# Fifteen small loads on ScalarE's DMA queue in a one-core decode layer

## The chip, the core and the metric

The kernel runs on one core of a Trainium2 chip. The metric is the device time of one execution in microseconds, as the median of the runs shown. A profiled execution has a time of its own, and a span (first to last instruction of the core) that is a little shorter.

## The reference, cut to what matters

One decode step of a transformer layer with adaptive layer norm, batch 2, width 640: attention with 32 heads of 192 over the last 1024 of 4096 cached positions, then a gated feed-forward of width 1536. Everything is bfloat16 in memory.

```python
mod = (silu(c) @ w_mod).reshape(2, 6, 1, 640)
sa, ca, ga, sb, cb, gb = (mod[:, i] for i in range(6))
h = layernorm(x) * (1 + ca) + sa
q = (h @ wq)                      # 32 heads x 192
p = softmax(q . k[-1024:] * 192 ** -0.5)
x = x + ga * ((p . v[-1024:]) @ wo)
h = layernorm(x) * (1 + cb) + sb
x = x + gb * ((gelu(h @ w_gate) * (h @ w_up)) @ w_down)
```

The cached keys and values that it reads are 50 MB, the weights some 27 MB; each byte is used once.

## The kernel before, in words

The program builds one list of operations for each engine (`_Sched`) and works out the waits from what each operation reads and writes. Within an engine the order is the order in which operations are added to its list. Line 257 (`k_dma`) is the one helper that issues every DMA, so all issues carry L257.

SyncE's list holds all large loads: w_mod, wq in two pieces, then the keys and values, then wo in four, w_gate, w_up in two, w_down in three pieces, and last the store of the output. Keys and values go through `ring`, five slots of 128 partitions x 24,576 bytes (64 of the 256 positions that a partition holds; a head occupies four partitions). The order of the 16 ring loads is the list `items`: four of k for batch 0, then v of batch 0 and k of batch 1 in turn, then v of batch 1. `declare_ring` puts a slot's next load into SyncE's list once the operation that empties the slot is in its own.

ScalarE's list begins with the two small loads of c into `cc` and x into `xc` (8 rows of 320 bytes each, L268 and L269), then silu of `cc` (L347), the evacuation of the modulation and of q. Line 434 is the last step of q: the copy of the selected q from PSUM into `qbc`, which the helper `move` records at L419. ScalarE's next operation after it is the exponential of the first softmax (L487), with the load of its function table before it.

After `qbc`, DVE multiplies each half slot of keys by q in place (L448), TensorE sums over parts of the head's width with an identity matrix (L459), DVE finishes the row sums (L468). `softmax` (L472 to L492) is a short chain over all engines. `d_mask` (L496) spreads the probabilities, `p_pv` (L508) multiplies them by the values. wo (L601), the second layer norm, w_gate and w_up (L617) and w_down (L638) follow, then two DVE operations (L644, L646) and the store. `filler` (L441) runs matmuls whose result nobody reads.

`sp_tail` at the end of SyncE's list waits for the store of the output.

Of the kernel before, what the change touches and what calls it, by code (L numbers as in the profile page):

```python
# [6 lines left out]
ACTF = mybir.ActivationFunctionType  # L7
# [96 lines left out]
def bass_adaLN_cond__sliding_block_cached__geglu_ffn__decode_kernel(  # L104
# [63 lines left out]
    with es:  # L168
        S = _Sched(nc, es)
# [35 lines left out]
        cc = sb("cc", [P, DN], BF16)  # L205
        sc = sb("sc", [P, DN], BF16)
# [21 lines left out]
        esum = sb("esum", [P, 2], F32)  # L228
        rden = sb("rden", [P, 2], F32)
        On = sb("On", [P, 2, Dh], BF16)  # L230
        ps = es.enter_context(nc.psum_tensor("ps", [P, 8, 512], F32))

        BK_T = 2
# [8 lines left out]
        def bank(k):  # L242
            return ("bank", k)
# [8 lines left out]
        sem_wd = [S.sem("d_wd%d" % i) for i in range(len(WD_SPLIT))]  # L252
        sem_ring = [S.sem("d_ring%d" % i) for i in range(NS)]
        sem_out = S.sem("d_out")

        def k_dma(dst, src):
            return lambda e: e.dma_start(dst, src)  # L257
# [5 lines left out]
        def dram_rows(v):  # L263
# [11 lines left out]
             reads=[("S", 0, 0), ("S", 0, 1), ("S", 1, 0), ("S", 1, 1)], writes=["ident_f"], name="ident_f")  # L275
        S.op("pool", lambda e: e.tensor_copy(out=ident_b[:, :], in_=ident_f[:, :]),
             reads=["ident_f"], writes=["ident_b"], name="ident_b")
# [3 lines left out]
             reads=["ident_f"], writes=["G32"], name="G32")  # L281
        S.op("dve", lambda e: e.tensor_reduce(out=M32[:, :], in_=ident_f[:, :].rearrange("p (h t) -> p h t", t=QP), axis=AX.X, op=ALU.add),
             reads=["ident_f"], writes=["M32"], name="M32")
        S.op("dve", lambda e: e.tensor_copy(out=M32b[:, :], in_=M32[:, :]), reads=["M32"], writes=["M32b"], name="M32b")
        S.op("dve", lambda e: e.tensor_copy(out=Bsel[:, :].rearrange("p (a m) -> p a m", m=SQ),
                                            in_=G32[:, :].unsqueeze(1).broadcast_to([P, NJ, SQ])),
             reads=["G32"], writes=["Bsel"], name="Bsel")

        S.op("dve", lambda e: e.tensor_copy(out=DS[:, :].rearrange("p (a m) -> p a m", m=SQ),
                                            in_=M32[:, :].unsqueeze(1).broadcast_to([P, NJ, SQ])),  # L290
             reads=["M32"], writes=["DS"], name="DS")


        for b in range(2):
            S.op("dve", (lambda b: lambda e: e.tensor_copy(
                out=SEL[:, b, :, BS * b:P:SQ], in_=G32[:, :].rearrange("p (j m) -> p m j", m=HM)))(b),
                reads=["G32"], writes=["SEL"], name="SEL%d" % b)
        for b in range(2):
            for m in range(HM):
                S.op("dve", (lambda b, m: lambda e: e.tensor_copy(  # L300
                    out=Qsel[:, b, m, :].rearrange("p (a m t) -> p a m t", a=NJ, m=HM)[:, :, m, :],
                    in_=ident_f[:, BS * b:P:SQ].unsqueeze(2).broadcast_to([P, NJ, QP])))(b, m),
                    reads=["ident_f"], writes=[("ring", 4, 0)], name="Qsel%d%d" % (b, m))
# [4 lines left out]
        def ring_keys(slot):  # L308
            return [half_key(slot, 0), half_key(slot, 1)]

        keep = {}
# [17 lines left out]
        def declare_ring(*consumed, upto=len(items)):  # L329
            ring_state["done"].update(place[it] for it in consumed)  # L330
            while ring_state["next"] < upto and (ring_state["next"] < NS or (ring_state["next"] - NS) in ring_state["done"]):
                n = ring_state["next"]
                kind, b, t = items[n]
                slot = n % NS
                cache = A_v_cache if kind == "v" else A_k_cache
                S.dma("sp", k_dma(ring[:, slot, :, :].rearrange("p j d -> p (j d)"),
                                  cache[b, :, K0:Sk, :].rearrange("h (q r) d -> h q r d", q=QP)[:, :, J * t:J * (t + 1), :].rearrange("h q r d -> h q (r d)")),
                      sem_ring[slot], writes=ring_keys(slot), name="ld_%s%d_%d" % (kind, b, t))
                ring_state["next"] += 1
# [4 lines left out]
        def to_contraction(dst, src, n, reads, writes, name):  # L344
            S.op("dve", lambda e: e.transpose(dst, src.rearrange("p (q k) -> p k q", k=n)), reads=reads, writes=writes, name=name)  # L345

        S.op("act", lambda e: e.activation(out=sc[:, :], in_=cc[:, :], func=ACTF.Silu), reads=["cc"], writes=["sc"], name="silu")  # L347
        to_contraction(scT[:, :, :], sc[:, :], KT, ["sc"], ["scT"], "scT")
        S.op("dve", lambda e: e.tensor_copy(out=X2[:, 0, :], in_=xc[:, :]), reads=["xc"], writes=[("X2", 0)], name="x_f32")  # L349

# [66 lines left out]
        def move(eng, dst, src, reads, writes, name):  # L417
            if eng == "act":
                S.op("act", lambda e: e.activation(out=dst, in_=src, func=ACTF.Copy), reads=reads, writes=writes, name=name)  # L419
            else:  # L420
                S.op("dve", lambda e: e.tensor_copy(out=dst, in_=src), reads=reads, writes=writes, name=name)  # L421
# [11 lines left out]
        S.op("pe", f, reads=[("qC", c) for c in range(NQC)] + ring_keys(4), writes=[bank(BK_O)], name="qsel")  # L433
        move("act", qbc[:, :, :].rearrange("p b d -> p (b d)"), ps[:, BK_O, 0:2 * Dh], [bank(BK_O)], ["qbc"], "qbc")
        declare_ring()

        def filler(n=1):
            def f(e):
                last = None
                for _ in range(n * ND):  # L440
                    last = e.matmul(ps[:, BK_W, 0:2 * Dh], lhsT=ident_b[:, :], rhs=qbc[:, :, :].rearrange("p b d -> p (b d)"),  # L441
                                    start=True, stop=True)
                return last
            S.op("pe", f, reads=["ident_b", "qbc"], writes=[bank(BK_W)], name="warm")
# [94 lines left out]
        steps = [(b, t, hf) for b in range(2) for t in range(NTL) for hf in range(2)]  # L539
# [29 lines left out]
        for i, nt in enumerate(OT_SPLIT):  # L569
            S.op("dve", (lambda t0, nt: lambda e: e.transpose(oT[:, t0:t0 + nt, :], oc.rearrange("p (q k) -> p k q", k=NT)[:, t0:t0 + nt, :]))(t0, nt),  # L570
                 reads=[("oc", c) for c in range(NQC)], writes=[("oT", t) for t in range(t0, t0 + nt)], name="oT%d" % i)
# [4 lines left out]
        for i, (ta, tb) in enumerate(wo_of):  # L576
# [5 lines left out]
              writes=["wg"], deps=r3_dead, name="ld_wg")  # L582
# [13 lines left out]
        for i, (ta, tb) in enumerate(wo_of):  # L596
            def f(e, ta=ta, tb=tb):
# [9 lines left out]
             reads=[bank(BK_M), ("modC", 0)], writes=[("lnt", 0)], name="ga_attn")  # L607
        S.op("dve", lambda e: e.tensor_tensor(out=X2[:, 0, :], in0=lnt[:, 0, :], in1=X2[:, 0, :], op=ALU.add),
             reads=[("lnt", 0)], writes=[("X2", 0)], name="x1")
        layer_norm("ln2", 1, 3)  # L610

        def ffn_gu(bk, wv, key, name, ka, kb):
            def f(e):
# [10 lines left out]
             reads=[bank(BK_G[0])], writes=["gl"], name="gelu")  # L624
        k0 = 0
        for ci, nk in enumerate(WU_SPLIT):
# [3 lines left out]
             reads=[bank(BK_G[1]), "gl"], writes=["aC"], name="geglu")  # L630
        to_contraction(aT[:, :, :], aC[:, :], FT, ["aC"], ["aT"], "aT")
        f0 = 0
        for ci, nf in enumerate(WD_SPLIT):
            def f(e, f0=f0, nf=nf):
# [10 lines left out]
             reads=[bank(BK_C), ("modC", 1)], writes=[("lnt", 1)], name="gb_y")  # L645
        S.op("dve", lambda e: e.tensor_tensor(out=sc[:, :], in0=lnt[:, 1, :], in1=X2[:, 0, :], op=ALU.add),  # L646
             reads=[("lnt", 1), ("X2", 0)], writes=["sc"], name="outC")
        S.dma("sp", k_dma(dram_rows(out[:, 0, :]), rows_of(sc)), sem_out, reads=["sc"], name="st_out")

        with nc.Block() as block:  # L650
            def sp_tail(e):
                e.wait_ge(sem_out, 16)

            @block.sync
            def _(e):
                S.emit("sp", e, tail=sp_tail)

            @block.gpsimd
            def _(e):
                S.emit("pool", e)  # L660

            @block.scalar
            def _(e):
                S.emit("act", e)

            @block.vector
            def _(e):
                S.emit("dve", e)

            @block.tensor  # L670
            def _(e):
                S.emit("pe", e)
# [28 lines left out]
```

## Time and profile before

| what | us |
|---|---|
| median of 3 runs | 189.07 (188.91 to 189.26) |
| the profiled execution | 188.59 |
| its span | 186.9 |
| DVE busy | 107.2 |
| PE busy | 121.0 |
| ScalarE busy | 13.9 |
| median from issue to landing, a ring load of keys | 29.6 |
| the same, a ring load of values | 25.3 |

The span moved 77.01 MB at a mean of 412 GB/s. Busy shares are means over stages with different limits; the DMA row of the slices, 40 slices of 4.67 us, tells for each stage whether loads were under way on all engines. Records of single DMA packets give a start, a duration, a size and a queue, but not which of the 16 DMA engines carried them; where one engine's packets are told apart below, it is because each starts where the one before it ended.

### The profile page before, as it was taken

To read this page: it belongs to the slowest core of one execution; us is meant where nothing else is said; L and a number is where in the kernel's file an instruction comes from. 1 tells how busy PE (TensorE), PEld (TensorE's weight loads), DVE (VectorE), ACT (ScalarE), POOL (GpSimd) and SP (SyncE) were. 2 spreads that over 40 slices of the span, in tenths; PEclk is the share of its full clock that TensorE was granted. 3 is DMA by queue.
4 is the path that set the end of the run, shared out by engine and by line. 5 is a ranking of instruction groups with operands and counts; after the bars stand their busy time and mean duration, and the time that the engine had idled before them with its cause. 6 is when DMAs were issued, how large, how long until landed. Compare 5 with 4: busy or idle time off the path is not lost.

```text
span 186.9 us, 2216 instructions
## 1 busy us (share of the span) xinstructions
PE 121.0 (65%) x982; PEld 60.5 (32%) x982; DVE 107.2 (57%) x114; ACT 13.9 (7%) x24; POOL 4.9 (3%) x12
## 2 busy tenths in 40 slices
PE   0004543565999889449999939929529997255442
PEld 0001221251343334125454513504225664244111
DVE  6802500029599998389599298288475612903331
ACT  2003200031000000000000000000010002400400
POOL 8100000000000000000000000000000000000000
PEclk9999999555699999966999997987957999955555
DMA  7999999999999999999999999999999999999980
GB/s 263 395 474 426 402 434 424 421 437 447 437 426 428 421 419 426 437 437 442 437 424 416 421 431 431 431 435 442 426 426 421 425 423 434 420 415 427 412 367 24
DMA packets 4220, 77.01 MB, mean 412 GB/s; under 512 B 500, under 2 KB 500, under 8 KB 1140
## 3 DMA queue, kind: packets, MB, share of 16 engines
q1 hardware_dynamic: 4188, 76.88, 96.6%
q8 instruction: 7, 0.11, 0.2%
q10 hardware_dynamic: 24, 0.01, 0.0%
q14 instruction: 1, 0.01, 0.0%
HBM read 76.88 MB, written 0.00 MB: 411 GB/s over the span
## 4 chain that ended last, share of the span: by engine, by line
DMA 48%; PE 27%; DVE 21%; SPq 2%; issue 1%; ACT 1%; DVEq 0%
DMA ring<-in_A_k_cache_dram 34%; DVE ring L448 14%; DMA ring<-in_B_w_down_dram 13%; PE ps L508 11%; PE ps L459 11%; PE ps L441 3%; DVE Sg L468 3%; DVE Em L496 2%; SPq L257 2%; ACT E_sb L487 1%; PE ps L638 1%; PE ps L489 1%; DVE M L474 0%; PE ps L483 0%; DVE gm L478 0%
## 5 line engine op out<-in xcount | busy, mean ns | idle before, releaser
L448 DVE TENSOR_TENSOR ring<-ring,qbc 128x6144 bf16<-128x6144 bf16 x16 | 53.5, 3351 | 10.8 <-DMA ring<-in_A_k_cache_dram 10.8
L459 PE MATMUL ps<-ring,ident_b 128*128 128x512 bf16 x192 | 49.8, 415 | 11.2 <-DVE ring L448 11.2
L459 PEld LDWEIGHTS ps<-ring,ident_b 128*128 128x128 bf16 x192 | 19.3, 105 | 38.9 <-DVE ring L448 15.4
L508 PE MATMUL ps<-ring,Em 128*64 128x384 bf16 x256 | 26.1, 365 | 4.9 <-DVE Em L496 4.9
L496 DVE TENSOR_TENSOR Em<-E_sb,M32b 128x2048 bf16<-128x2048 bf16 x8 | 18.2, 2282 | 4.0 <-PE ps L508 4.0
L508 PEld LDWEIGHTS ps<-ring,Em 128*64 128x64 bf16 x256 | 15.4, 122 | 14.9 <-DVE Em L496 6.4
L441 PE MATMUL ps<-qbc,ident_b 128*128 128x384 bf16 x88 | 18.1, 335 | 0.7 <-ACT qbc L419 0.7
L468 DVE TENSOR_REDUCE Sg<-ps 128x32 f32<-128x512 f32 x16 | 11.0, 687 | 8.8 <-PE ps L459 8.8
L388 PE MATMUL ps<-ring,scT 128*32 128x480 bf16 x40 | 4.4, 601 | 15.0 <-DMA ring<-in_w_mod_dram 15.0
L411 PE MATMUL ps<-r,hT 128*32 128x384 bf16 x80 | 6.7, 518 | 8.7 <-DMA r<-in_A_wq_dram 8.7
L441 PEld LDWEIGHTS ps<-qbc,ident_b 128*128 128x128 bf16 x88 | 8.1, 100 | 9.8 <-issue 4.5
L421 DVE CAST ring<-ps 128x384 bf16<-128x384 f32 x4 | 2.0, 553 | 15.4 <-PE ps L411 14.5
L601 PE MATMUL ps<-r,ring 128*32 128x160 bf16 x192 | 5.9, 304 | 5.8 <-DMA r<-in_A_wo_dram 3.0
L601 PEld LDWEIGHTS ps<-r,ring 128*32 128x32 bf16 x192 | 5.1, 128 | 6.6 <-DMA r<-in_A_wo_dram 3.6
L411 PEld LDWEIGHTS ps<-r,hT 128*32 128x32 bf16 x80 | 3.0, 140 | 12.4 <-issue 6.1
L522 ACT ACTIVATE On<-ps,rden 32x192 bf16<-32x192 f32 x4 | 1.6, 412 | 71.0 <-PE ps L508 61.4
L388 PEld LDWEIGHTS ps<-ring,scT 128*32 128x32 bf16 x40 | 1.3, 132 | 16.3 <-DVE X L349 14.9
L526 DVE TENSOR_SCALAR On<-ps,rden 32x192 bf16<-32x192 f32 x4 | 1.7, 418 | 7.4 <-ACT On L522 7.4
L617 PE MATMUL ps<-ring,hT 128*32 128x384 bf16 x40 | 3.7, 519 | 3.3 <-DVE hT L345 2.6
L570 DVE STREAM_TRANSPOSE ring<-ring 128x512 bf16<-128x512 bf16 x3 | 4.1, 1430 | 0.1
L606 DVE TENSOR_TENSOR lnt<-ps,modC 128x160 f32<-128x160 f32 x1 | 0.3, 325 | 6.5 <-PE ps L601 6.5
L487 ACT ACTIVATE E_sb<-Sg,nb 128x256 bf16<-128x256 f32 x2 | 1.0, 508 | 40.7 <-DVE nb L486 40.7
(68 smaller groups left out, 57.2 us busy)
## 6 DMA issues: line engine op xcount, KB each, us to landing
ring<-in_A_k_cache_dram SPq DMA_DIRECT2D x8, 3072.0 KB, 29.6
ring<-in_A_v_cache_dram SPq DMA_DIRECT2D x8, 3072.0 KB, 25.3
r<-in_A_wo_dram SPq DMA_DIRECT2D x2, 2560.0 KB, 38.1
ring<-in_w_mod_dram SPq DMA_DIRECT2D x1, 4800.0 KB, 14.0
r<-in_A_wq_dram SPq DMA_DIRECT2D x1, 4608.0 KB, 24.5
r<-in_A_wq_dram SPq DMA_DIRECT2D x1, 3072.0 KB, 32.4
r<-in_A_wo_dram SPq DMA_DIRECT2D x1, 1920.0 KB, 44.0
ring<-in_B_w_gate_dram SPq DMA_DIRECT2D x1, 1920.0 KB, 18.2
```

Source lines behind the costliest of these rows:

```text
L257: return lambda e: e.dma_start(dst, src)
L388: last = e.matmul(ps[SQ * j:SQ * j + SQ, bk, 0:3 * DN].rearrange("p (i n) -> p i n", i=3), lhsT=scT[:, k, :], rhs=wm_v[:, k, 3 * part * D: ...
L411: last = e.matmul(ps[SQ * j:SQ * j + SQ, BK_H + c, 0:QC], lhsT=hT[:, k, :], rhs=wq_v[:, k, RN * j + QC * c:RN * j + QC * (c + 1)], start=( ...
L441: last = e.matmul(ps[:, BK_W, 0:2 * Dh], lhsT=ident_b[:, :], rhs=qbc[:, :, :].rearrange("p b d -> p (b d)"), start=True, stop=True)
L448: S.op("dve", lambda e: e.tensor_tensor(out=ring[:, ks, hf * JH:(hf + 1) * JH, :], in0=ring[:, ks, hf * JH:(hf + 1) * JH, :], in1=qbc[:, b ...
L459: last = e.matmul(o_ap, lhsT=ident_b[:, :], rhs=ring[:, ks, hf * JH:(hf + 1) * JH, ci * GC:(ci + 1) * GC], start=(ci == 0), stop=(ci == NC ...
L468: S.op("dve", lambda e: e.tensor_reduce(out=S_sb[:, a:a + JH], in_=ps[:, hf, 0:JH * GC].rearrange("p (j c) -> p j c", j=JH), axis=AX.X, op ...
L496: S.op("dve", lambda e: e.tensor_tensor(out=Em[:, t % 2, :, :], in0=E_sb[:, J * t:J * (t + 1)].unsqueeze(2).broadcast_to([P, J, H]), in1=M ...
L508: last = e.matmul(ps[r:r + 2 * H, BK_O, 0:ON], lhsT=Em[:, t % 2, 2 * jp:2 * jp + 2, :].rearrange("p j c -> p (j c)"), rhs=ring[:, vs, 2 * ...
L570: S.op("dve", (lambda t0, nt: lambda e: e.transpose(oT[:, t0:t0 + nt, :], oc.rearrange("p (q k) -> p k q", k=NT)[:, t0:t0 + nt, :]))(t0, n ...
L601: last = e.matmul(ps[SQ * j:SQ * j + SQ, BK_M, 0:DN], lhsT=oT[:, t, :], rhs=wo_v[:, t, DN * j:DN * j + DN], start=(t == 0), stop=(t == NT ...
L617: last = e.matmul(ps[SQ * j:SQ * j + SQ, bk, 0:FN], lhsT=hT[:, k, :], rhs=wv[:, k, FN * j:FN * j + FN], start=(k == 0), stop=(k == KT - 1) ...
```

## The change

Behind the evacuation into `qbc` and the ring loads that `declare_ring` adds there, ScalarE's list gets 15 DMA loads. Load i (0 to 14) takes the first 2(i + 1) elements of x, as i + 1 rows of two bfloat16 elements (4 bytes), into rows 0 to i of `cc`, columns 2i and 2i + 1. `cc` has been read by silu before, which the loads name as a dependency, and nobody reads it afterwards. All 15 count on one new semaphore, for which SyncE waits at the very end.

```diff
+        NST = 15
...
+        sem_st = S.sem("d_steps")
...
-        S.op("act", lambda e: e.activation(out=sc[:, :], in_=cc[:, :], func=ACTF.Silu), reads=["cc"], writes=["sc"], name="silu")
+        keep["silu"] = S.op("act", lambda e: e.activation(out=sc[:, :], in_=cc[:, :], func=ACTF.Silu), reads=["cc"], writes=["sc"], name="silu")
...
         move("act", qbc[:, :, :].rearrange("p b d -> p (b d)"), ps[:, BK_O, 0:2 * Dh], [bank(BK_O)], ["qbc"], "qbc")
         declare_ring()
+
+
+        for i in range(NST):
+            S.dma("act", k_dma(cc[0:i + 1, 2 * i:2 * i + 2], A_x[0, 0, 0:2 * (i + 1)].rearrange("(k n) -> k n", n=2)),
+                  sem_st, writes=[("steps", i)], deps=[keep["silu"]], name="ld_step%d" % i)
...
             def sp_tail(e):
                 e.wait_ge(sem_out, 16)
+                e.wait_ge(sem_st, 16 * NST)
```

## The prediction

> **What bounds the kernel now.** I read the page's slices and queues first, then busy shares by stage, the chain that ended last, ScalarE's timeline, and the trace's records of single DMA packets (start, duration, bytes, queue).
>
> ```profile
> DMA  7999999999999999999999999999999999999980
> GB/s 263 395 474 426 402 434 424 421 437 447 437 426 428 421 419 426 437 437 442 437 424 416 421 431 431 431 435 442 426 426 421 425 423 434 420 415 427 412 367 24
> ...
> q1 hardware_dynamic: 4188, 76.88, 96.6%
> q8 instruction: 7, 0.11, 0.2%
> q10 hardware_dynamic: 24, 0.01, 0.0%
> ```
>
> The 16 DMA engines are busy from the second slice to the last but two. q1 is SyncE's queue and carries all but 0.13 of the 77.01 MB. q10 is ScalarE's: today only the loads of c and x. q8 fetches instructions, seven packets of 16 KB.
>
> ```profile
> 41.00:50.00 9.00, 6.51 (x16) 2.22 (x17) 6.63 (x2) 1.65 (x2) 0.00 (x0) 0.50 1.01 434
> 50.00:58.00 8.00, 7.48 (x37) 3.33 (x35) 7.79 (x5) 0.00 (x0) 0.00 (x0) 1.00 1.03 440
> 58.00:79.00 21.00, 17.07 (x79) 7.40 (x79) 17.84 (x15) 0.00 (x0) 0.00 (x0) 1.00 1.00 428
> 79.00:122.00 43.00, 36.39 (x230) 17.86 (x230) 31.85 (x17) 1.01 (x3) 0.00 (x0) 0.88 1.00 429
> ```
>
> The last two columns are the DMA share and GB/s. The share is 1.00 or a little more (records overlap slightly), so the queue is never empty, though DVE and PE also have busy stages. The ends of the chain say the same:
>
> ```profile
> 2.25 39.16 DMA ring<-in_A_k_cache_dram
> ...
> 97.16 24.82 DMA ring<-in_A_k_cache_dram
> ...
> 157.71 25.00 DMA ring<-in_B_w_down_dram
> 182.71 0.04 issue
> 182.75 0.73 PE ps L638 x15
> 183.48 0.04 issue
> 183.52 0.49 PE ps L638 x8
> ```
>
> A load lands some 25 us after its issue, because that much is queued ahead of it. The last piece of w_down lands at 183.48; behind it lie 3.4 us (8 matmuls, two DVE operations, the store) to the end of the span at 186.9. A later SyncE issue is therefore free up to tens of us, while every ns put into the slowest DMA engine moves the end.
>
> **How the engines stand to each other.** In the packet records a row of 24,576 bytes takes 912 ns, and the next one on the same engine starts 908 to 913 ns after it. The 16 completions of the last w_down load spread over 1.95 us, from 181.53 to 183.48: eight engines within 0.69 us of the first, eight 1.21 to 1.95 us behind it. The late ones had been pushed back, one at a time, by the 16 KB fetches and one of 8 KB (in the first such case the fetch took 945 ns, and the engine's next data packet 1,421 instead of 912). The two slowest are 0.02 us apart, the next 0.15 ahead of these.
>
> **The change part by part.** Nothing is removed. Added are 15 loads behind qbc's evacuation in ScalarE's order, one semaphore, and one wait at the end of SyncE's list.
>
> ```profile
> 1.06 1.10 ACTq L257 DMA_DIRECT2D cc<-in_c_dram  x1
> 2.20 0.55 ACTq L257 DMA_DIRECT2D xc<-in_A_x_dram  x1
> ...
> 40.88 0.49 ACT L419 ACTIVATE qbc<-ps 128x384 bf16<-128x384 f32 x1 [3.06 <-PE ps L430]
> 41.38 1.28 ACT L487 ACT_TABLE_LOAD   x1
> 79.06 0.51 ACT L487 ACTIVATE E_sb<-Sg,nb 128x256 bf16<-128x256 f32 x1 [36.39 <-DVE nb L486]
> ```
>
> *Issue on ScalarE.* One issue took 0.55 and 1.10 us; 15 take 8.3 to 16.5. They begin at 41.4 and end at 49.7 to 57.9, and the 1.28 us table load for the exponential now comes behind them (at 59.2 at the latest). ScalarE's next work waits for DVE until 79.06, so at least 19.9 us of idle time hide all of it: 0. If that cover were gone, the exponential, the mask at L496 and PV would be late by as much. The dependency on silu is met (silu ran at 10.15). No one reads cc after silu, and nobody waits for the new semaphore before the end. SyncE's list is not reordered.
>
> *Packets.* q10 now shows 24 packets: 16 rows of 320 bytes and 8 packets of 4 bytes. Two loads with 8 completion packets mean four engines per load: the destination has 8 rows, the DRAM side is 4 by 2. The new loads have r rows on both sides, so I take r engines for a load of r rows, one 4-byte row and one 4-byte completion each: 120 + 120 packets; the first engine gets 15 loads, the next 14, the last none. (The Trainium skill, DMA: Bandwidth & Descriptors, section "Why a DMA increments its semaphore by 16 and not by 1", says that the engine count is the largest number up to 16 that divides both outer dimensions, and that the lowest-numbered engines are used; the four completions per load agree with it, which engines these are the trace does not tell.)
>
> *Price of a packet.* The records of q10 show it, since c and x went in turn with w_mod's rows: on one engine a 320-byte packet began at 6.728 and w_mod's next row at 6.747; a 4-byte completion at 8.161, the next row at 8.167; again 320 bytes at 9.583, the row at 9.600. So 4 bytes of completion cost the big stream 6 ns, and 320 bytes 17 to 19. A 4-byte data row lies between 6 and 19 by the nearest rows; I take 9, nearer to the packet of the same size. A load costs each engine that it touches 9 + 6 = 15 ns (12 to 25). Drained in turn with 912 ns rows, the first engine's 30 packets take 30 x 0.92 = 27.6 us, so all have landed by about 70.
>
> *What reaches the end.* Only the slowest engine counts, and its place among the 16 is not to be seen. It gets 0 to 15 of the loads, on average 7.5: 7.5 x 15 ns = 0.11 us; bounds 0 and 15 x 25 = 0.38 us. The engines 0.15 us ahead of it can take over only with a few more loads, which lies within these bounds.
>
> *The added wait.* SyncE waits for a semaphore that was full 110 us before. By the smallest pieces of the chain (0.02 to 0.05 us) I take 0.05; 0 to 0.1.
>
> Sum: 0.11 + 0.05 = 0.16 us. The profiled execution took 188.59 us, 186.9 of span and 1.69 around it, so it becomes 188.75. It lies 0.48 under the median of the runs, 189.07; on that the forecast is 189.23, up 0.08%. Bounds of the sum (0 to 0.48) and the spread of the runs (-0.16, +0.19) give its own range, 188.9 to 189.6.
>
> **The rivals.**
>
> *Slower: a 4-byte row costs an engine a stall, not 9 ns.* The place is the slowest engine between 41 and 70 us. From far rows: the packet after an instruction fetch took 509 ns too much, one of 320 bytes costs 17 to 19. Between ends so far apart I take the geometric middle, about 98 ns. With 7.5 loads that is 7.5 x (98 + 6) = 0.78 us, plus 0.05: 189.9. It decides from about 38 ns a row (7.5 x 44 = 0.33, plus 0.05). Against it: behind c's and x's packets w_mod's rows run on at 1,420 ns, only two nearby ones at 1,453 and 1,469. For it: none of those packets was as small a data row. (The Trainium skill, DMA: Bandwidth & Descriptors, section "Specifications", gives 512 bytes as the least size for full rate and a read-modify-write below it; by that rule all 120 rows pay. The 320-byte rows, under the limit too, show 17 to 19 ns.)
>
> *Not the stated staircase: each load's rows on one engine.* Then one engine gets 120 rows and 15 completions, 120 x 6 to 19 + 0.09 = 0.81 to 2.37 us, middle 1.6. Against its own lead, about 1.0 us for an engine in the middle of the spread, 0.6 is left: 189.7 with the wait. Against it: the four completions per load above.
>
> *ScalarE stuck.* If each issue waited for the load before to land, 15 x (2 x 0.92 + 0.6) = 36.6 us put ScalarE at 78.0, and with the table load at 79.3, 0.2 behind the exponential's start. The 25 us of queued loads hide that again; only if an issue took over 3 us would it show, at some 0.5 us: 189.6. c and x, issued within 1.1 us of each other with neither landed until about 10, speak against it.
>
> *Faster: the staircase sets the engines out of step and their rows pass more evenly.* The ring's loads land 7.30 us apart on the leading engine, while eight rows of 0.908 and a completion would take 7.27. All of that, 0.03 on 17 rounds, would be 0.5 us: 188.6. Against it: the completions of one load already spread over 0.66 us at 25 us and 1.7 us from 32 us on, and the 7.30 does not change as they drift.
>
> **How the numbers follow.** Forecast 0.60; stall per row 0.19; one engine 0.06; ScalarE stuck 0.03; faster 0.12. About 0.2% (0.38 us) is what a measurement of this kernel can tell from no change. So faster 0.12, same 0.60, slower 0.28. The time is the forecast's, 189.2. The range goes from the faster rival, 188.6, to just past the stall's 189.9, at 190.0; what is outside is the upper half of the stalls and the far ends of the others, about 2 in 10.
>
> **What would show it.** q10 should hold 24 + 240 = 264 packets (with one engine per load 24 + 135 = 159). ScalarE's issues should end before 58, the exponential still start near 79, and no DMA share from 41 to 156 fall under 1.00. The last w_down piece should land 0 to 0.4 later than 183.48 against the span's start, with 3.4 us behind it. I am wrong if the next big row starts far more than 6 to 19 ns after a 4-byte row (stall), if ring loads land less than 7.29 us apart after 70 us (faster), or if the end moves by over 0.4 us while all landings stand.

## The result, and the profile after

| | before | changed |
|---|---|---|
| median of 20 runs, us | 188.94 (188.66 to 189.52) | 189.61 (189.19 to 190.41) |
| profiled execution, us | 188.59 | 189.35 |
| its span, us | 186.9 | 187.6 |
| last w_down piece landed, us from the span's start | 183.48 | 184.23 |

The ratio is 1.0035, 95% interval 1.0023 to 1.0047: slower by 0.67 us in the medians. The measured time lies in the stated range of 188.6 to 190.0, and 0.01 us outside the forecast's own range of 188.9 to 189.6; "within 0.2%", which had a chance of 0.60, did not come; "slower" had 0.28.

From the page of the changed kernel, its GB/s in 40 slices of 4.69 us and ScalarE's DMA queue:

```profile
GB/s 254 402 472 424 409 424 417 440 440 440 424 362 426 402 430 435 435 440 430 424 423 435 424 445 435 430 412 424 435 430 445 433 415 424 414 416 429 413 384 21
...
q10 hardware_dynamic: 264, 0.01, 0.1%
```

The twelfth slice, 51.6 to 56.3 us, fell from 426 to 362 GB/s, the fourteenth from 421 to 402. 264 packets are the 24 of before and 240 new ones.

Busy time by stage of the changed kernel (again the last two columns are DMA share and GB/s):

```profile
41.00:50.00 9.00, 6.22 (x22) 2.54 (x23) 7.33 (x4) 1.53 (x2) 0.00 (x0) 0.81 1.02 437
50.00:58.00 8.00, 7.39 (x36) 3.23 (x35) 8.00 (x5) 0.00 (x0) 0.00 (x0) 1.00 0.97 394
58.00:66.00 8.00, 7.09 (x35) 3.07 (x34) 8.00 (x5) 0.00 (x0) 0.00 (x0) 1.00 1.00 417
66.00:79.00 13.00, 9.35 (x45) 4.13 (x43) 8.95 (x9) 0.60 (x2) 0.00 (x0) 1.00 1.00 431
```

The stream loses speed between 50 and 66 us only. Two longer stretches show it, first before, then the changed kernel:

```profile
50.00:66.00 16.00, 14.48 (x70) 6.41 (x69) 15.79 (x9) 0.00 (x0) 0.00 (x0) 1.00 1.02 435
66.00:150.00 84.00, 65.85 (x404) 32.30 (x404) 61.32 (x42) 2.03 (x6) 0.00 (x0) 0.88 1.00 429
...
50.00:66.00 16.00, 14.48 (x70) 6.30 (x69) 16.00 (x9) 0.00 (x0) 0.00 (x0) 1.00 0.99 406
66.00:150.00 84.00, 65.26 (x392) 31.68 (x392) 59.84 (x41) 2.03 (x6) 0.00 (x0) 0.88 1.00 430
```

Over the 16 us it ran at 406 GB/s instead of 435, which is 29 x 16 = 464 KB, or 1.1 us at 430 GB/s. In the packet records most of the lost time is not in the small packets: each takes 7 to 9 ns, 0.13 us in all on an engine. It is in the keys' and values' rows beside them: between 44 and 70 us, 99 rows of 24,576 bytes took over 930 ns instead of 912. Two of them follow an instruction fetch, as the only two of before do. The other 97 took up to 1,181 ns, and what they took beyond 912 adds up to 0.58 us on an engine. Half of the 99 took 996 ns and more.

ScalarE's timeline of the changed kernel:

```profile
40.76 0.49 ACT L421 ACTIVATE qbc<-ps 128x384 bf16<-128x384 f32 x1 [3.05 <-PE ps L432]
40.76 5.32 ACTq L259 DMA_DIRECT2D cc<-in_A_x_dram  x15
46.11 1.28 ACT L494 ACT_TABLE_LOAD   x1 [4.87 <-issue]
78.14 0.51 ACT L494 ACTIVATE E_sb<-Sg,nb 128x256 bf16<-128x256 f32 x1 [30.74 <-DVE nb L493]
```

All 15 issues are over by 46.1, and the exponential still waits for DVE until 78.14, 0.92 earlier than before (79.18 in the second profile of this kernel, e8). ScalarE costs nothing. The end of the chain of waits:

```profile
158.28 25.20 DMA ring<-in_B_w_down_dram
183.47 0.04 issue
183.52 0.73 PE ps L645 x15
184.24 0.03 issue
184.28 0.49 PE ps L645 x5
```

It is the old end, 0.76 us later.

*A measure for the experiments.* For each ring load, take the mean time of its 16 completions and subtract that of before's profile; the difference between the sixth ring load (landed at 77) and the first (landed at 40, ahead of any small packet) is what the small loads took from an engine on average. Below it is called the net delay: 0.85 us in the changed kernel, 0.85 x 16 / 120 = 113 ns for each row and its completion. The expectations quote 0.91, which has the 0.06 us of the first load in it. How steady the measure is shows in e9, which has no small load under way at 77 us: 0.01.

### The profile page after: what moved, and what is told of

Same layout as the page of the kernel before. It is cut to its first block, busy times and chain, and to the rows that moved or that the text cites. A ratio compares the mean times of both kernels' runs of the same rounds, so it can differ in the third digit from the quotient of the medians.

```text
span 187.6 us, 2232 instructions
## 1 busy us (share of the span) xinstructions
PE 121.0 (64%) x982; PEld 60.6 (32%) x982; DVE 107.1 (57%) x114; ACT 13.9 (7%) x24; POOL 4.9 (3%) x12
## 4 chain that ended last, share of the span: by engine, by line
DMA 48%; PE 24%; DVE 23%; SPq 2%; issue 1%; ACT 1%; DVEq 0%
DMA ring<-in_A_k_cache_dram 35%; DVE ring L455 16%; DMA ring<-in_B_w_down_dram 13%; PE ps L515 11%; PE ps L466 8%; PE ps L448 3%; DVE Sg L475 3%; DVE Em L503 2%; SPq L259 2%; ACT E_sb L494 1%; PE ps L645 1%; DVE M L481 0%; PE ps L496 0%; PE ps L490 0%; DVE gm L485 0%
## 5 line engine op out<-in xcount | busy, mean ns | idle before, releaser
L466 PE MATMUL ps<-ring,ident_b 128*128 128x512 bf16 x192 | 48.4, 406 | 12.2 <-DVE ring L455 12.2
L515 PE MATMUL ps<-ring,Em 128*64 128x384 bf16 x256 | 27.1, 374 | 4.9 <-DVE Em L503 4.9
```

The costliest lines, as they stand in the source:

```text
L466: last = e.matmul(o_ap, lhsT=ident_b[:, :], rhs=ring[:, ks, hf * JH:(hf + 1) * JH, ci * GC:(ci + 1) * GC], start=(ci == 0), stop=(ci == NC ...
L515: last = e.matmul(ps[r:r + 2 * H, BK_O, 0:ON], lhsT=Em[:, t % 2, 2 * jp:2 * jp + 2, :].rearrange("p j c -> p (j c)"), rhs=ring[:, vs, 2 * ...
```

## The experiments

All change only the small loads; e8 changes nothing. The 15 loads of 1 to 15 rows are called the staircase. The diffs are shortened, and `<-` stands between a load's destination and its source. Ratios are to before on the same chip, with 95% intervals. "Long rows" are rows of 24,576 bytes above 930 ns between 44 and 70 us; in every run two of them follow an instruction fetch.

| run | what the loads read | ratio | long rows | net delay us |
|---|---|---|---|---|
| changed | 60 bytes of x, shared | 1.0035 (1.0023 to 1.0047) | 99 | 0.85 |
| e8 | the same again | 1.0028 (1.0012 to 1.0044) | 64 | 0.68 |
| e5 | 60 bytes of w_mod, shared | 1.0048 (1.0028 to 1.0068) | 69 | 0.65 |
| e11 | rows 32 bytes apart | 1.0017 (1.0001 to 1.0034) | 45 | 0.46 |
| e6 | rows 64 bytes apart | 1.0006 (0.9990 to 1.0023) | 9 | 0.14 |
| e12 | a place for each load | 1.0007 (0.9994 to 1.0021) | 2 | 0.11 |
| e1 | 120 distant rows | 1.0008 (0.9993 to 1.0024) | 3 | 0.11 |
| e2 | one load, 120 rows of x | 1.0025 (1.0010 to 1.0040) | 22 | 0.16 |
| e3 | 15 loads of one row | 1.0000 (0.9980 to 1.0019) | 2 | 0.02 |
| e4 | rows of 320 bytes | 1.0006 (0.9995 to 1.0017) | 25 | 0.26 |
| e7 | the staircase twice | 1.0045 (1.0029 to 1.0061) | 69 | 0.81 |

### e1: other addresses

```diff
-A_x[0, 0, 0:2 * (i + 1)].rearrange("(k n) -> k n", n=2)
+w_mod[a:a + i + 1, 0:2]        # a = i * (i + 1) // 2
```

> The same 15 loads, but each of the 120 rows is read from another row of w_mod (7,680 bytes apart) instead of the first 60 bytes of x, which all loads of the change share. In the changed kernel the 16 completions of a ring load come on average 0.91 us later than before once the small loads are through (about 113 ns for each row and its completion), mostly as rows of 24,576 bytes that took up to 1,155 ns instead of 912. Theory A (a 4-byte row costs the engine that carries it, whatever it reads): mean delay again 0.8 to 1.0 us, time again 0.5 to 0.8 us over before. Theory B (all engines read one and the same place in memory and hold each other up there): mean delay under 0.3 us, time within 0.3 us of before.

Theory B holds, A falls: with the same loads, rows, completions, issues, destinations and the same wait, the hold-up is gone. The page of this run (GB/s in slices of 4.68 us) has no dip in its twelfth slice (the 378 in its fifth lies ahead of the small loads, so a single slice is weak evidence; the packet records carry the argument):

```profile
GB/s 263 395 442 457 378 457 419 420 441 436 447 431 422 426 419 420 426 426 447 447 424 426 426 420 426 420 445 452 426 426 431 411 430 429 428 405 433 407 363 21
```

What is left, 0.11 us on an engine, is 0.11 x 16 / 120 = 15 ns for a row with its completion.

### e2: one load

```diff
-for i in range(15): cc[0:i + 1, 2 * i:2 * i + 2] <- i + 1 rows of x
+cc[0:120, 0:2] <- A_x[0, 0, 0:240] as 120 rows
```

> One load of 120 rows of 4 bytes instead of 15 loads with 120 rows in all: the rows stay, the completions fall from 120 to some 15, the issues from 15 to 1. Theory A (the rows cost): mean delay of the ring loads stays at 0.8 to 1.0 us. Theory C (the completions or the issues cost, not the rows): mean delay falls to about 15/120 of it, 0.1 us, and the time is within 0.2 us of before. Theory B gives as much as A or more, since all rows read 480 bytes of x close together.

None of the three theories gives this run's net delay of 0.16 us and its time of 1.0025 together. A falls again (0.8 expected), and C had fallen in e1, which has all completions and issues. The packets are 159 = 24 + 120 + 15, so 15 engines took 8 rows each; 20 of its 22 long rows lie between 49 and 54 us, nearly all of them while the engines read the same 480 bytes. Beyond the packets (8 rows of 9 ns on each engine, 0.07 us) that leaves 0.09 us to the shared place, less than B said. But the profiled execution, at 188.77 us, was the fastest of the 12; their median is 0.43 us over before's, so the 0.16 need not be typical of this run.

### e3: one engine alone

```diff
-cc[0:i + 1, 2 * i:2 * i + 2] <- A_x[0, 0, 0:2 * (i + 1)]
+cc[0:1, 2 * i:2 * i + 2] <- A_x[0, 0, 2 * i:2 * i + 2]
```

> 15 loads of one row each, 15 rows and 15 completions, all on one engine. Theory A: that engine is late by 15 x 0.113 = 1.7 us, the others by nothing, mean delay 0.11; the end moves by what is left after the engine's lead over the slowest one (0 to 1.7 us; if it is one of the leading eight, 0 to 0.5). Theory C gives the same here. Theory B: mean delay and the engine's own delay both near 0 (one engine alone reads the place), time within 0.2 us of before.

54 packets, 30 of them new, and nothing moves: the net delay is 0.02 us, where 15 x 15 ns on one engine would give 0.014. A stall of 113 ns a row by size alone is out.

### e4: wider rows

```diff
-cc[0:i + 1, 2 * i:2 * i + 2] <- 4-byte rows of x
+cc[a:a + i + 1, :] <- w_mod[0, 0:160 * (i + 1)] as rows of 160   # a = i * (i + 1) // 2
```

> The same 15 loads and 120 rows, but each row is 320 bytes (from the first row of w_mod) into a row of its own of the unread tile. If the small size is what costs (a partial write of a few bytes): no more than the changed kernel, and less if 320 bytes are written more cheaply. By the rows of c and x, 17 to 19 ns each and 6 for a completion: mean delay 120 x 25 / 16 = 0.19 us, time within 0.3 us of before. Theory A with a price by row, not by bytes: mean delay 0.8 to 1.1 us. Theory C: the same as the changed kernel, 0.9.

320 bytes a row, 320 bytes apart: net delay 0.26 us, 35 ns for a row and completion (20 ns is the record of such a row). The 20 long rows between 58 and 66 us are 931 to 948 ns, not 1,000 and more. Eighty times the bytes cost a third of the changed kernel's delay, and e1's rows of 4 bytes still less, so a small size is not what costs.

### e5 and e6: is it x, or the sharing

```diff
-A_x[0, 0, 0:2 * (i + 1)].rearrange("(k n) -> k n", n=2)
+w_mod[0, 0:2 * (i + 1)].rearrange("(k n) -> k n", n=2)                   # e5
+w_mod[0, 0:32 * (i + 1)].rearrange("(k n) -> k n", n=32)[:, 0:2]         # e6
```

> The 15 loads as in the change, but the shared place is the first 60 bytes of w_mod instead of x. With rows from 120 distant rows of w_mod the time was 1.0008 of before and the mean delay of the ring loads 0.17 us. Theory B (many engines read one and the same place): mean delay again 0.7 to 1.0 us, dozens of rows of 24,576 bytes above 930 ns between 50 and 66 us, time 0.4 to 0.9 us over before. Rival (something about the tensor x, such as where it lies): no stretched rows, mean delay under 0.25 us, time as with the distant rows.

> Row j of every load is read from 64 x j bytes into w_mod's first row, so that rows of one load lie 64 bytes apart (960 bytes in all) and each engine reads a place of its own again and again. If the shared 60 bytes themselves are the trouble (one small unit of memory, read by many engines): few or no stretched rows, mean delay 0.15 to 0.3 us, time within 0.3 us of before. If nearness within a kilobyte or one engine's repeated reads are enough: as in the change, mean delay 0.7 to 1.0 us, 0.4 to 0.9 us over before. The single load of 120 rows from 480 bytes of x lay between (0.25 us, 20 stretched rows).

e5 behaves as the change does, so it is not x. The twelfth slice of its page shows 377:

```profile
GB/s 262 393 441 456 401 437 417 424 445 440 424 377 421 417 430 435 430 424 435 430 444 419 435 435 419 430 423 440 435 430 435 416 424 428 420 423 415 415 375 16
```

e6 reads 960 bytes of the same row of w_mod with 64 bytes between rows and costs little more than distant rows. Nearness and repeated reading by one engine are not enough.

### e11: two engines on 64 bytes

```diff
+w_mod[0, 0:16 * (i + 1)].rearrange("(k n) -> k n", n=16)[:, 0:2]
```

> Row j of every load from 32 x j bytes of w_mod's first row, so that two engines share each 64 bytes; at 64 bytes apart there were 5 stretched rows in the 50 to 66 us and 0.17 us of mean delay, at 4 bytes apart 65 and 0.76. If a unit of 64 bytes is what is shared, and two engines already disturb each other: 0.25 to 0.5 us, 10 to 40 stretched rows. If the unit is 32 bytes or less, or only many engines on one unit hurt: as at 64 bytes apart, under 0.25 us.

Rows 32 bytes apart: 0.46 us and 45 long rows, between 4 bytes apart (0.65) and 64 (0.14). So two engines in one 64 bytes already disturb each other, and if what they share is a unit of fixed size, it is larger than 32 bytes. Whether it ends at 64 is open: e6 still has seven long rows that follow no fetch.

### e12: at the same moment

```diff
-w_mod[0, 0:2 * (i + 1)]
+w_mod[i, 0:2 * (i + 1)]
```

> Each load reads its rows from a place of its own: load i from the first bytes of w_mod's row i (7,680 bytes apart), its rows 4 bytes apart as in the change. So the engines share a place within one load and not between loads. One engine has a turn for a small packet every 0.92 us, and at any moment the engines stand at different loads of the staircase. If what counts is that engines read one place at the same moment of their turns: almost no stretched rows, mean delay 0.15 to 0.25 us, time within 0.3 us of before. If a load's rows are read together when it is issued, or repetition is not needed: mean delay 0.5 to 0.9 us, 30 to 70 stretched rows, time 0.3 to 0.9 us over before.

Within a load the rows stand 4 bytes apart as in e5; only different loads no longer share a place. The hold-up is gone: 0.11 us, two long rows (the two of before), every small packet at 9 ns. So in the staircase a place has to be shared between loads (e12 against e5) and by several engines (e3, e6). Why that is so can be argued from the order: an engine's small packets take turns with 912 ns rows, so at any moment the engines on the staircase stand at different loads, and in e12 at different places. That the reads meet in time was not measured. And one load can be enough: e2's 20 long rows came while each engine read eight rows of the same 480 bytes. Stages of e12, to be read against those of the changed kernel:

```profile
50.00:58.00 8.00, 7.39 (x36) 3.17 (x35) 8.00 (x5) 0.00 (x0) 0.00 (x0) 1.00 1.03 434
58.00:66.00 8.00, 7.09 (x35) 3.09 (x34) 8.00 (x5) 0.00 (x0) 0.00 (x0) 1.00 0.99 423
```

The DMA share is 1.03 and 0.99, the rate 434 and 423 GB/s against 394 and 417 in the changed kernel.

### e8, e7, e9, e10: how steady, how much, when

e8 is the changed kernel again. e7 has 30 loads (the staircase twice in a row). e9 issues the staircase behind the first exponential instead of behind `qbc`; e10 does both.

```diff
                     softmax(0)
+                    for i in range(0, 15):      # e9; e10: range(15, 30), and 0 to 14 at the old place
+                        r = i % 15 + 1
+                        S.dma("act", ... cc[0:r, 2 * i:2 * i + 2], A_x[0, 0, 0:2 * r] ...)
```

> The changed kernel once more, for a second profile. Its times spread wider (189.19 to 190.41) than those of before, so if the hold-up depends on how the engines happen to stand: mean delay other than 0.91 us, between 0.6 and 1.3, again with 60 or more rows above 930 ns between 50 and 66 us; the last landing later by 0.2 to 1.2 us than before. If it is fixed: 0.85 to 0.95 us and a last landing 0.7 to 0.8 us later.

> The staircase of the change twice, 30 loads with 240 rows, from the same 60 bytes of x. Theory B with a price by row (113 ns a row and completion): mean delay 1.6 to 2.0 us, time 1.1 to 1.9 us over before. If the price grows with the number of loads under way at once: over 2.2 us of mean delay. If it is a single upset at the start: still 0.9 us.

> The 15 loads of the change, from the same 60 bytes of x, but issued behind the first softmax's exponential (near 79 us) instead of behind q's evacuation; the large loads under way are then others (values and keys of 80 to 107 us). In the changed kernel the stretched rows lay between 50 and 66 us. If the shared place is all that matters: dozens of rows above 930 ns between 84 and 105 us, mean delay of the ring loads from 110 us on 0.6 to 1.0 us, time 0.3 to 0.9 us over before. If it takes the particular keys that are loaded between 50 and 66 us: no stretched rows, mean delay 0.15 to 0.25 us, time within 0.3 us.

> Both: the staircase at its place in the change and once more behind the exponential (near 79 us). Doubled in one place it cost no more than once (0.91 us of mean delay instead of the 1.8 expected; no stretched row after 66 us). If the hold-up ends by itself because the engines have been pushed out of step: the second staircase adds only its packets, 0.1 to 0.2 us, mean delay 0.9 to 1.2 us in all. If each staircase of its own meets the same trouble: 1.5 to 2.0 us in all, time 0.9 to 1.8 us over before.

e8 gave 0.68 us net and a last landing 0.62 later: the loss differs by execution. e7 took 0.81, no more than one staircase (the last of its three expectations), though its small packets went on until 93 us with shared reads all along; no long row but one behind a fetch after 64. A price by row fails there.

e9 has its long rows (43, one of them behind a fetch) between 92 and 106 us, net delay 0.41 us at the loads landed after 110, and 1.0011 (0.9995 to 1.0027) in time, which does not tell it from before. Both are under what was expected (0.6 to 1.0 us of delay, 0.3 to 0.9 us of time), but the long rows are there, so no particular keys are needed. e10 lost 0.70 in the first staircase and 0.39 in the second, as e9 alone, and its time is 1.0060 (1.0038 to 1.0082, 7 runs). The sum lies in the band expected of engines pushed out of step, but a second staircase lost as much as a late one alone, with 45 long rows (one behind a fetch), so that theory is not borne out. GB/s of e10, slices of 4.70 us:

```profile
GB/s 261 393 471 423 447 389 443 439 423 434 423 408 399 423 411 439 429 434 439 376 437 439 418 429 423 439 432 444 418 429 418 434 430 436 406 421 431 412 360 16
```

Two dips, 408 and 399 in the twelfth and thirteenth slice and 376 in the twentieth (89.3 to 94.0 us), lie where the long rows are; the 389 in the sixth lies ahead of all small loads. Still open: why the hold-up starts late (6 us behind the first small packets in the changed kernel, 11 in e9), why it ended in e7 while reads went on, and why it is smaller later. What in the way to the memory makes shared reads slow was not looked into either.

## Why the prediction was right or wrong

*The bound* was right: the DMA stream sets the end, and the last w_down piece's delay (0.75 us) is the span's.

*Issue on ScalarE* was right in its effect and dear in its price: an issue took 243 to 405 ns, not 550 to 1,100, and 30.7 us of idle time were left.

*Packets* came as said: 264, and 159 when 120 rows came in one load. The rule of the Trainium skill on the engine count (DMA: Bandwidth & Descriptors, section "Why a DMA increments its semaphore by 16 and not by 1") agrees also there: the largest number up to 16 that divides 120 is 15, and 15 completions were seen. Rival "one engine" falls with it.

*Price of a packet* is the step that failed: 15 ns for a row and its completion. As the price of packets it was exact: e1 and e12 gave 15. But it was read from c's and x's loads, whose engines each read rows of their own, and carried over to loads that all read the same 60 bytes. There the price was 113 ns, and the other 98 did not lie in the small packets: the greater part of it is found in the big rows beside them (0.58 of the 0.85 us), the rest the records do not tell apart. The diff showed the shared address; no row of the profile of before had one, and no rival was put on it. The sign that the prediction named, a DMA share under 1.00 between 41 and 156 us, came (0.97 from 50 to 58 us), but it is a weak one: before itself has 0.98 from 98 to 106 us. The long rows are the clear one.

*What reaches the end* inherited the error: 0.11 us with an upper bound of 0.38, measured 0.75. How it got there is more than an average. From 71 to 145 us the slowest engine's completions were only 0.25 us late, since the loss fell mostly on engines with a lead. Then came the instruction fetch at 148.98 us. It cost its engine 1.55 us, and that engine was only 1.1 us ahead of the slowest; none was more than 1.4 ahead, where before it had been up to 2.0. From the next load on the last completion was 0.75 late. Before, the same fetch fell on an engine 1.8 us ahead and moved nothing at the end. Which engine it falls on is luck: in e12, without the hold-up, it fell on one 1.4 us ahead and made the last completion 0.36 late. So the 0.75 of this one profile is not all the hold-up's; what the hold-up costs is shown by the medians of the runs, 0.67 us here, and in e12 nothing that can be told from before (1.0007).

*The range* held by luck. Its upper end, 190.0, came from the stall rival; the forecast's own sum, 0.16 us with bounds of 0 to 0.48, does not reach the 0.67 us of the medians.

*The added wait* cannot be told apart: e1 and e12 hold it and the issues, and stay within 0.24% at their intervals' ends.

*The stall rival* had nearly the size (98 and 6 ns a row) with a wrong reason. It was the rule of 512 bytes (the Trainium skill, the same page, section "Specifications") that gave it its mechanism; e12 and e1 have the same 4-byte rows at 15 ns, and e4's 320-byte rows, under the limit too, cost 35, so a read-modify-write of that kind shows no price here beyond these 15 and 35 ns. *ScalarE stuck* and *faster* fell: the ring's loads land 7.31 us apart from 77 to 121 us.

## What to carry to other kernels

Price a small transfer by what else reads the same place while it is under way, not by its bytes alone: 120 rows of 4 bytes cost an engine 0.11 us on average when the loads read different places, and 0.65 to 0.85 when several engines and loads kept reading the same 60 bytes. Where a DMA stream bounds the kernel, look at the big rows beside a small load and not only at the load, and follow the slowest engine: a delay that only shortens an engine's lead comes out when something else, here an instruction fetch, needs that lead.

## What the runs showed of the hardware

Reads of 4 bytes by many engines from one place delayed rows that the same engines fetched from elsewhere, in the changed kernel by up to 269 ns a row (912 to 1,181). The loss fell with the distance of the rows: net 0.65 us at 4 bytes (e5), 0.46 at 32 (e11), 0.14 at 64 (e6), 0.11 at 7,680 (e1, where no two loads share a row either). In the profile of before, eight of the 16 engines end 1.21 to 1.95 us behind the first, and that spread is mostly made by single fetches of instructions. One fetch cost its engine some 1.6 us (1,018 ns for itself and 540 more for the row behind it, before at 148.96 us). So a mean delay reaches the end in part or in whole: in the changed kernel 0.25 us of 0.85 up to 145 us, 0.75 after one more fetch.
